# The product of the inverse with the betas on VectorE in all six sets, with the order of all engines drawn anew

## The chip, the cores and the metric

The program runs on one core of a Trainium2 chip. A core has TensorE (PE in the profile; its weight loads are PEld), VectorE (DVE), ScalarE (ACT), GpSimd (POOL) and SyncE (SP), which here issues the transfers. The metric is the device time of one execution in microseconds (us), as the median of several runs.

## What is computed

Three stages follow one another: a delta-rule attention over 4 batches, 8 heads, 768 tokens and head size 48, a gated MLP with a convolution of 5 taps, and a second gated MLP with a mixing over the tokens. Cut to the first stage, to which the change belongs, and the shapes of the others:

```python
k_n = k / (norm(k, axis=-1) + 1e-6)
for t in range(768):
    y[:, :, t] = q[:, :, t] @ state
    v_old = state^T k_n[:, :, t]
    state = state + beta[:, :, t] * outer(k_n[:, :, t], v[:, :, t] - v_old)

gate = sigmoid(causal_conv5(x, conv_w));  x1 = (gate * (x @ w_val)) @ w_out        # x: [4, 768, 384]
h = gelu_tanh(x1 @ w_in);  u, v = halves(h);  v_n = layernorm(v) * g_ln            # 512 each
out = x1 + (u * (w_sg @ v_n + b_sg)) @ w_out2
```

## The kernel before

**Attention.** The tokens are cut into chunks of 64, 12 for each of the 4 batches, 48 in all, and two chunks (`d`) are prepared together. Within a chunk the delta rule becomes the inverse of a triangular matrix made of the products of keys, times the betas. The inverses are computed for blocks of 32 tokens, all 32 blocks of four pairs of chunks in one go: this is a *set*, `k`, of which there are six. For a set, `norm`, `keys` and `gram` make the keys and their products `gd`, and `base(k)` inverts. `X` [128 partitions, 32 x 32, float32] starts as the transposed `gd`, and VectorE eliminates it in 30 steps, larger ones as a product into `tmp` and an addition, small ones in fused instructions (`X<-X`). Then `X` is multiplied by `bm`, the betas with the upper triangle kept, and transposed twice into `tab`, from which `tbh` and `tah` come (a float16 value and its remainder; for set 0 one of the transposes goes to `w2`). In the kernel before, the multiplication by `bm` is VectorE's in set 0 and GpSimd's in sets 1 to 5 (line 873).

`merge(d)` joins two 32-blocks to a 64-block with matmuls into `ps_b` and puts the result into `tbd`. Then `seq(n)` runs chunk after chunk, a recurrence: PE multiplies keys with the state (`ps_q<-wh,kj`), for batches 1 to 3 VectorE adds the values (`ps_q<-ps_q,vf`), ScalarE and VectorE split the result into two float16 parts (`rh`), PE multiplies by the inverse (`ps_q<-rh,tbd`), ScalarE and VectorE split again (`wh`), PE updates the state (`ps_state<-wh,kj`) and both split it once more (`wh<-ps_state`). `attend(n)` makes the outputs (`ps_y`, `mh`, `ys`).

**MLPs.** For each batch three tiles of 256 tokens go through `front`, `value`, `hidden`, `gates`, `mix` and `final`, with matmuls into `ps_mlp` of 256 or 512 columns. They need the attention's output of their tokens, so most of them come late. Each float32 product is made of three float16 matmuls. `a`, `gvh`, `gth`, `v`, `vnh`, `xh` and `st` are MLP tiles.

**The order.** All code of the kernel only records operations. `in_order` (line 110) then issues each engine's operations in the order that a table written out by hand, `ORDER` (line 239), gives for that engine: numbers of its operations in recorded order, with `a:n` for a run of n. Each engine works its list strictly in turn. The list of VectorE before has one operation for set 0's product, and five fewer than after. Where the planner's costs foresee a gap of PE, it adds *fillers*, matmuls into an unused half of `ps_state` (`ps_state<-minus`), 64 or 128 rows high. All transfers are on SP's queue.

The touched lines, and the two beside them:

```python
nc.vector.tensor_tensor(out=rows, in0=rows, in1=t, op=ALU.add)                               # elimination
(nc.vector if k == 0 else nc.gpsimd).tensor_tensor(out=X, in0=X, in1=bm, op=ALU.mult)        # line 873
nc.vector.transpose(out=t, in_=src)                                                          # tab<-X
```

Of the kernel before, what the change touches and what calls it, by code (L numbers as in the profile page):

```python
# [15 lines left out]
ALU = mybir.AluOpType  # L16
# [196 lines left out]
class Pool:  # L213
# [5 lines left out]
    def tile(self, shape, dtype, name, tag=None, **kw):  # L219
# [326 lines left out]
def kernel(  # L546
# [17 lines left out]
    nc = Program(tc)  # L564
# [276 lines left out]
    def base(k):  # L841
# [6 lines left out]
        X = pp.tile([P, 32, 32], F32, name="X", tag="f4", bufs=2)  # L848
# [4 lines left out]
        bm = pp.tile([P, 32, 32], F32, name="bm", tag="xb")  # L853
# [4 lines left out]
        for j in range(1, 31):  # L858
            m = 31 - j
            if min(j, m) <= FUSED:  # L860
                for a, i in ((a, i) for a in range(j if j <= m else 1) for i in range(1 if j <= m else m)):
                    if j <= m:
                        t, row, c = X[:, a, j + 1:32], X[:, j, j + 1:32], X[:, a, j:j + 1]
                    else:
# [5 lines left out]
                                    in1=X[:, j:j + 1, j + 1:32].to_broadcast([P, j, m]), op=ALU.mult)  # L870
# [525 lines left out]
```

## Time and profile before

| | us |
|---|---|
| median of 3 runs | 645.57 (643.87 to 649.93) |
| profiled execution, its own time | 646.62 |
| its span, first to last instruction | 644.7 |
| PE busy | 575.0 (89%) |
| DVE busy | 503.1 (78%) |
| ACT busy | 398.2 (62%) |
| POOL busy | 179.6 (28%) |

A busy share is the time in which an engine has at least one instruction under way. The view of stretches gives for each engine the busy time and, as (x...), the instructions that begin there, then PE's granted clock as a share of full speed. The order of time has, for each row, the start, the duration, the engine, what is written from what, and in brackets the idle time ahead of it with what ended it. A row that stands for several instructions has their number at x. All lines are L108, since one helper issues everything: tiles tell the rows apart.

### The profile page before, as it was taken

To read this page: it belongs to the slowest core of one execution; us is meant where nothing else is said; L and a number is where in the kernel's file an instruction comes from. 1 tells how busy PE (TensorE), PEld (TensorE's weight loads), DVE (VectorE), ACT (ScalarE), POOL (GpSimd) and SP (SyncE) were. 2 spreads that over 40 slices of the span, in tenths; PEclk is the share of its full clock that TensorE was granted. 3 is DMA by queue.
4 is the path that set the end of the run, shared out by engine and by line. 5 is a ranking of instruction groups with operands and counts; after the bars stand their busy time and mean duration, and the time that the engine had idled before them with its cause. 6 is when DMAs were issued, how large, how long until landed. Compare 5 with 4: busy or idle time off the path is not lost. (4 is left out here: it accounts for less than half of the span.)

```text
span 644.7 us, 23559 instructions
## 1 busy us (share of the span) xinstructions
PE 575.0 (89%) x9821; PEld 473.8 (73%) x9821; DVE 503.1 (78%) x1341; ACT 398.2 (62%) x932; POOL 179.6 (28%) x204
## 2 busy tenths in 40 slices
PE   0678879779979989799999999889999999999997
PEld 0555446668767767688888689778978897877886
DVE  7898998979889998988999879899887854562222
ACT  7886697756876767775466785344948544524221
POOL 7404041126423625366001650001605010303000
PEclk9999998989999998999999999999999999999999
DMA  7664367877579776687678778788687763211121
GB/s 223 160 202 132 126 189 235 186 156 165 107 182 175 134 122 146 128 195 132 163 143 179 145 123 170 121 140 152 120 155 141 107 142 102 63 50 34 58 82 50
DMA packets 288826, 89.22 MB, mean 138 GB/s; under 512 B 250704, under 2 KB 276944, under 8 KB 288720
## 3 DMA queue, kind: packets, MB, share of 16 engines
q1 hardware_dynamic: 288720, 87.72, 63.0%
q8 instruction: 77, 1.26, 0.9%
q14 instruction: 29, 0.24, 0.1%
HBM read 51.81 MB, written 23.33 MB: 117 GB/s over the span
## 5 line engine op out<-in xcount | busy, mean ns | idle before, releaser
L108 PE MATMUL ps_mlp<-wg,vnh 128*128 128x256 f16 x864 | 112.4, 272 | 1.4 <-DVE ps_mlp L108 1.4
L108 PEld LDWEIGHTS <-vnh 128*128 128x128 f16 x864 | 80.5, 97 | 12.0 <-issue 2.1
L108 PEld LDWEIGHTS <-kj 112*128 112x128 f16 (+1 forms) x1632 | 69.2, 97 | 21.4 <-issue 12.7
L108 PEld LDWEIGHTS <-kc 64*64 64x64 f16 x1920 | 42.1, 113 | 47.5 <-DVE kc L108 20.8
L108 PE MATMUL ps_mlp<-gvh,wi 128*128 128x256 f16 x432 | 58.0, 272 | 1.2 <-ACT v L108 0.8
L108 PE MATMUL ps_mlp<-gth,w 128*128 128x256 f16 x432 | 58.8, 272 | 0.0
L108 DVE TENSOR_TENSOR tmp<-X 128x84 f32<-128x84 f32 (+12 forms) x156 | 56.1, 360 | 1.4
L108 DVE TENSOR_TENSOR X<-X,tmp 128x84 f32<-128x84 f32 (+12 forms) x156 | 54.5, 349 | 1.5
L108 PE MATMUL ps_mlp<-wi,gvh 128*128 128x512 f16 x216 | 54.7, 379 | 0.6 <-ACT gvh L108 0.4
L108 DVE SCALAR_TENSOR_TENSOR ps_mlp<-ps_mlp,gl,bs 128x256 f32<-128x256 f32 x48 | 23.4, 488 | 34.3 <-PE ps_mlp L108 33.9
L108 DVE SCALAR_TENSOR_TENSOR a<-x,cw,a 128x256 f32<-128x256 f32 x108 | 48.8, 486 | 1.6 <-ACT a L108 1.3
L108 PE MATMUL ps_mlp<-xh,wv 128*128 128x256 f16 x324 | 45.7, 272 | 2.2 <-ACT xh L108 2.1
L108 PE MATMUL ps_mlp<-gvh,wo 128*128 128x256 f16 x324 | 47.1, 272 | 0.1
L108 PEld LDWEIGHTS <-m1p 128*128 128x128 f16 x1152 | 39.5, 96 | 9.9 <-issue 5.7
L108 PE MATMUL pk<-i,kc 64*64 64x64 f16 x704 | 22.5, 200 | 27.2 <-DVE kc L108 20.0
L108 PEld LDWEIGHTS <-wi 128*128 128x128 f16 x432 | 40.3, 97 | 6.4 <-issue 1.3
L108 PEld LDWEIGHTS <-w 128*128 128x128 f16 x432 | 40.8, 98 | 5.0
L108 PE MATMUL ps_y<-qh,kj 112*128 112x64 f16 x576 | 32.8, 193 | 4.2 <-ACT ys L108 4.1
L108 POOL TENSOR_TENSOR X<-X,bm 128x1024 f32<-128x1024 f32 x5 | 11.8, 2353 | 87.4 <-DVE X L108 72.0
L108 PEld LDWEIGHTS <-ws 128*128 128x128 f16 (+1 forms) x828 | 32.2, 98 | 4.9 <-issue 3.2
L108 PEld LDWEIGHTS <-wo 128*128 128x128 f16 x342 | 31.8, 97 | 5.5 <-issue 0.9
L108 POOL TENSOR_TENSOR vnh<-v,vnh 128x512 f16<-128x512 f32 x24 | 27.9, 1170 | 25.6 <-ACT vnh L108 25.5
(165 smaller groups left out, 1451.5 us busy)
## 6 DMA issues: line engine op xcount, KB each, us to landing
keys_d<-kc SPq DMA_DIRECT2D x22, 512.0 KB, 4.1
kj<-keys_d SPq DMA_DIRECT2D x44, 256.0 KB, 5.0
wg<-wgd SPq DMA_DIRECT2D x12, 768.0 KB, 4.8
ws<-wh SPq DMA_DIRECT2D x66, 96.0 KB, 3.6
qf<-in_qt SPq DMA_DIRECT2D x24, 224.0 KB, 3.5
kf<-in_kn SPq DMA_DIRECT2D x12, 384.0 KB, 4.7
vf<-in_vn SPq DMA_DIRECT2D x24, 192.0 KB, 3.4
xd<-ys SPq DMA_DIRECT2D x48, 96.0 KB, 3.0
```

The lines of the kernel that those rows point to most:

```text
L108: op.call()
```

## The change

In sets 1 to 5 the product of `X` with `bm` is made by VectorE, as in set 0. VectorE's list has 5 operations more, GpSimd's 5 fewer. The table of order is drawn anew for all five engines. One line of each list of VectorE stands for it:

```diff
     vector=(
-        "1 5 0 4 6 3 2 7 47:2 8:2 248 10 414 11 249 156 12 415 13 147 14 157 15 158 16 152 17 153 18 154 19:6 161 25 "
+        "2:2 1 0 4:4 47:2 8:2 248 10:2 415 12:2 156:2 249 14 416 158 15 152 16 153 147 17 154 18:7 161 25 33 162 28 "
...
-        (nc.vector if k == 0 else nc.gpsimd).tensor_tensor(out=X, in0=X, in1=bm, op=ALU.mult)
+        nc.vector.tensor_tensor(out=X, in0=X, in1=bm, op=ALU.mult)
```

VectorE at the end of set 1's inverse, before, from the `rh` of a chunk of batch 0 on (`wh_111` and `wh_110` are two of the three tiles of split states, `tbd_95` one of the two of merged inverses, `rs_t`, `rs` and `wst` norms of later keys and weights):

```order
L108 SCALAR_TENSOR_TENSOR rh<-ps_q,rh 128x192
L108 TENSOR_TENSOR mh<-ps_y,mh 128x256
L108 SCALAR_TENSOR_TENSOR tbd_95<-ps_b,tbd_95 32x8x32
L108 SCALAR_TENSOR_TENSOR wh_111<-ps_q,wh_111 128x4x48
L108 STREAM_TRANSPOSE tab<-X 128x1024
L108 TENSOR_SCALAR rs<-rs_t 128x32
L108 SCALAR_TENSOR_TENSOR wh_111<-ps_state,wh_111 112x4x48
```

The same place in the changed kernel:

```order
L108 SCALAR_TENSOR_TENSOR rh<-ps_q,rh 128x192
L108 TENSOR_TENSOR X<-X,bm 128x1024
L108 TENSOR_TENSOR mh<-ps_y,mh 128x256
L108 SCALAR_TENSOR_TENSOR wh_111<-ps_q,wh_111 128x4x48
L108 STREAM_TRANSPOSE tab<-X 128x1024
L108 TENSOR_SCALAR rs<-rs_t 128x32
L108 SCALAR_TENSOR_TENSOR tbd_95<-ps_b,tbd_95 32x8x32
L108 SCALAR_TENSOR_TENSOR gx<-pk,gx 128x256
L108 SCALAR_TENSOR_TENSOR rs_t<-rs 128x32
L108 SCALAR_TENSOR_TENSOR wst<-wst 128x384
L108 SCALAR_TENSOR_TENSOR wh_111<-ps_state,wh_111 112x4x48
```

The product comes in behind `rh`; `tbd`, `gx`, `rs_t` and `wst` stand ahead of the split of the state, `wh_111<-ps_state`, where before only `rs` stood between it and the transpose.

VectorE at the end of set 2's inverse, before, from the split of a state of batch 1 on:

```order
L108 SCALAR_TENSOR_TENSOR wh_109<-ps_state,wh_109 112x4x48
L108 TENSOR_TENSOR gvh<-ps_mlp,gvh 128x512
L108 SCALAR_TENSOR_TENSOR ps_q<-ps_q,vf 128x192
L108 SCALAR_TENSOR_TENSOR ps_mlp<-a,ps_mlp 128x256
L108 SCALAR_TENSOR_TENSOR rh<-ps_q,rh 128x192
```

The same place in the changed kernel:

```order
L108 SCALAR_TENSOR_TENSOR wh_109<-ps_state,wh_109 112x4x48
L108 TENSOR_TENSOR X<-X,bm 128x1024
L108 TENSOR_TENSOR gvh<-ps_mlp,gvh 128x512
L108 SCALAR_TENSOR_TENSOR ps_q<-ps_q,vf 128x192
L108 SCALAR_TENSOR_TENSOR ps_mlp<-a,ps_mlp 128x256
L108 SCALAR_TENSOR_TENSOR rh<-ps_q,rh 128x192
```

Here the product stands ahead of the whole row from `gvh` to `rh`, which are in the same order as before.

## Rows read from the trace of the kernel before

**Rows 1.** The page: span, and part 1, busy us and share.

```profile
span 644.7 us, 23559 instructions
...
PE 575.0 (89%) x9821; PEld 473.8 (73%) x9821; DVE 503.1 (78%) x1341; ACT 398.2 (62%) x932; POOL 179.6 (28%) x204
```

**Rows 2.** Stretches: length, busy us of PE, PEld, DVE, ACT, POOL, clock, DMA.

```profile
140.00:200.00 60.00, 53.79 (x1348) 44.84 (x1345) 52.42 (x145) 44.81 (x107) 27.46 (x28) 1.00 0.74 175
200.00:273.00 73.00, 64.66 (x1292) 53.03 (x1290) 66.90 (x189) 51.25 (x125) 33.77 (x35) 0.98 0.73 131
273.00:345.00 72.00, 71.70 (x1224) 62.66 (x1223) 66.01 (x180) 44.74 (x104) 22.87 (x22) 1.00 0.79 163
345.00:480.00 135.00, 127.93 (x2212) 109.01 (x2211) 117.91 (x308) 83.56 (x197) 34.27 (x31) 1.00 0.79 141
480.00:600.00 120.00, 118.51 (x1528) 99.78 (x1527) 69.84 (x175) 61.25 (x135) 22.08 (x24) 1.00 0.44 93
```

**Rows 3.** Tile X: count, shortest, median, longest ns, first and last start.

```profile
L108 POOL TENSOR_TENSOR X<-X,bm x5: 2346/2353/2358, 140.1 to 448.2; 128x1024 f32<-128x1024 f32 x5
L108 DVE TENSOR_TENSOR X<-X,bm x1: 1226/1226/1226, 80.1 to 80.1; 128x1024 f32<-128x1024 f32 x1
```

**Rows 4.** Order of time on DVE, end of set 1: start, duration us.

```profile
139.68 0.26 DVE L108 SCALAR_TENSOR_TENSOR X<-X 128x30 f32<-128x30 f32 x1
...
140.47 0.36 DVE L108 SCALAR_TENSOR_TENSOR rh<-ps_q,rh 128x192 f16<-128x192 f32 x1
140.81 0.42 DVE L108 TENSOR_TENSOR mh<-ps_y,mh 128x256 f16<-128x256 f32 x1
141.27 0.42 DVE L108 SCALAR_TENSOR_TENSOR tbd<-ps_b,tbd 32x256 f16<-32x256 f32 x1
141.74 0.36 DVE L108 SCALAR_TENSOR_TENSOR wh<-ps_q,wh 128x192 f16<-128x192 f32 x1
142.47 1.25 DVE L108 STREAM_TRANSPOSE tab<-X 128x1024 f32<-128x1024 f32 x1 [0.38 <-POOL X L108]
...
144.15 0.36 DVE L108 SCALAR_TENSOR_TENSOR wh<-ps_state,wh 112x192 f16<-112x192 f32 x1 [0.36 <-PE ps_state L108]
```

**Rows 5.** Waits of PE over the span: us in all, times, longest.

```profile
PE ps_b L108 <- DVE tbh L108: 1.0, 1, 1.0
```

**Rows 6.** Order of time on DVE: rh after set 2, two products gd.

```profile
152.28 1.81 DVE L108 SCALAR_TENSOR_TENSOR gd<-gd,beta_sb 128x1024 f32<-128x1024 f32 x1
...
205.91 0.36 DVE L108 SCALAR_TENSOR_TENSOR rh<-ps_q,rh 128x192 f16<-128x192 f32 x1
...
210.65 1.21 DVE L108 SCALAR_TENSOR_TENSOR gd<-gd,beta_sb 128x1024 f32<-128x1024 f32 x1
```

**Rows 7.** Order of time on PE after set 2.

```profile
204.91 1.81 PE L108 MATMUL ps_mlp<-wi,gvh 128*128 128x512 f16 x7
206.56 0.46 PE L108 MATMUL ps_q<-rh,tbd 128*128 128x48 f16 x12
```

**Rows 8.** Order of time on PE where 64 and 128 rows alternate.

```profile
353.95 0.34 PE L108 MATMUL pk<-i,kc 64*64 64x64 f16 x9
354.23 0.25 PE L108 MATMUL ps_state<-wh,kj 128*128 128x48 f16 x3
354.40 0.31 PE L108 MATMUL pk<-i,kc 64*64 64x64 f16 x7
354.64 0.40 PE L108 MATMUL ps_state<-wh,kj 128*128 128x48 f16 x9
```

**Rows 9.** Order of time on POOL beside the first product gd.

```profile
152.20 0.82 POOL L108 TENSOR_TENSOR tah<-tab,tah 128x256 f16<-128x256 f32 x1
```

**Rows 10.** Stretches of one microsecond at two falls of the clock.

```profile
134.00:135.00 1.00, 0.00 (x0) 0.00 (x0) 0.97 (x5) 0.40 (x1) 0.00 (x0) 0.88 0.06 5
248.00:249.00 1.00, 1.00 (x26) 1.00 (x24) 0.71 (x2) 0.96 (x3) 1.00 (x2) 0.50 0.55 63
```

**Rows 11.** Tile ps_state: the fillers.

```profile
L108 PE MATMUL ps_state<-minus x268: 269/272/421, 20.5 to 273.0; 128*128 128x256 f16 x70, 64*64 64x256 f16 x64
```

392 rows, old and new, of tables (gpsimd, scalar, sync, tensor) are left out of this document.

## The prediction

> **What bounds the kernel now.** I read the page first, then the table by stretches, then the waits, and last the order of time around the instructions that move. The page gives a span of 644.7 us with TensorE (PE) busy for 89% of it [rows 1]. The table by stretches splits this into two regimes. From 273 us on PE is busy for 71.70 of 72, 127.93 of 135 and 118.51 of 120 us: it is the bound there, and VectorE (DVE) and GpSimd (POOL) work only counts if PE runs dry. Before that PE has 53.79 of 60 and 64.66 of 73 us, while DVE has 52.42 and 66.90 us: 87% and 92% [rows 2]. There neither is at its limit alone. The recurrence over the chunks goes PE, ScalarE, VectorE and back to PE several times in each chunk, and VectorE squeezes the inverses and everything else between its steps. PE's remaining gaps are partly filled by idle matmuls of the planner, so its busy share there overstates useful work.
>
> Counted over the whole order, the program has 267 such fillers before and 252 after. In both, the last one is issued when the same share of the real matmuls is still to come. What PE has to do after it is thus the same, and the time can only change by when PE gets there and by its stalls behind that place. The last filler begins at 273.0 us [rows 11], which is why I cut the table there.
>
> **The change, part by part.**
>
> *Removed.* Five POOL multiplications X·bm of 2.353 us, 11.8 us in all [rows 3]. POOL is busy for 28% of the span [rows 1], so its own time is worth nothing. A gain could only come from a shorter way from the end of the inverse to its users. In the second set, the first that changes, the inverse ends at 139.68 + 0.26 = 139.94 us and its transposition starts at 142.47 [rows 4], 2.5 us later. The new instruction is 1.1 us shorter, but the order shown above puts two instructions of the recurrence between it and the transposition, as before. And nobody waits: of PE's waits only one, 1.0 us, is for a product of an inverse, and it is for set 0, which VectorE made already [rows 5]. I cost this gain at 0. What hides it is the matmuls of earlier chunks, which PE still has; without them it would be at most 1.1 us a set.
>
> *Added.* Five VectorE multiplications. Set 0 shows the very form: 1.226 us [rows 3], so 5 × 1.226 = 6.1 us of VectorE. Where do they lie? POOL's five begin at 140, 204, 275, 354 and 448 us (first and last in [rows 3]); three of them are behind the last filler, where PE has work queued and is 95 to 100% busy [rows 2]: 0, hidden by PE's matmuls of the MLPs. Without that cover each would cost up to 1.2 us.
>
> Two remain. **Set 1 (140 us).** Before, VectorE does rh, mh, tbd, wh, idles 0.38 us until POOL is done, and transposes [rows 4]. After, the multiplication stands between rh and mh, and tbd goes behind the transposition together with three more instructions ahead of the next wh (from ps_state). Placing the new rows with the old durations: rh ends its turn at 140.81, the multiplication holds the engine to about 142.0, mh and wh to 142.6, the transposition to 143.8, then rs, tbd, gx, rs_t and wst about 1.5 us more: wh from ps_state starts at about 145.3 instead of 144.15 [rows 4], so the recurrence is late by some 1.1 us. PE idles at this very place for DVE's wh already. Bounds 0 (the next chunk catches up) and 1.2; I take 1.1, since fillers still run there and PE has little else.
>
> **Set 2 (204 us).** The multiplication stands ahead of gvh, ps_q and rh. rh began at 205.91 and its matmuls at 206.56 [rows 6, 7]; 1.2 us later is 207.8. PE covers this with matmuls on wi that end at 206.56 [rows 7], and the new order has no more of them in front of the matmuls of rh. So PE idles for about 1.2 us more; bounds 0 (the 64.66 of 73 us leave 8 us of idle time nearby that may shrink in return) and 1.2. I take 1.2. Together +2.3 us.
>
> *Redrawn order.* The other rows of the table moved by a few places; I compared the lead between maker and user for the recurrence and the merges along PE's order, and no class of them is systematically shorter. One count differs: matmuls of 64 rows and of 128 rows alternate 167 times before and 147 times after; behind the last filler 38 and 32. In the trace, from 353.95 to 354.40 us, 9 matmuls of 64 rows and 3 of 128 rows take 0.45 us. The spacing inside the groups is (0.34 - 0.19)/8 = 0.019 and (0.40 - 0.18)/8 = 0.027 us, so 0.25 us is theirs and 0.20 us belongs to two alternations: 0.10 us each [rows 8]. Six fewer where PE is the bound give -0.6 us; the other 14 lie where PE waits anyway, worth between 0 and -1.4; I take -0.7, the half. The 15 fillers that go are time in which PE waited: 0.
>
> *POOL's other work.* Without the 2.35 us, qh and vnh of POOL can start earlier. Their users are on PE's list for later; 0.
>
> *Sum.* 2.3 - 0.6 - 0.7 = +1.0 us. The profiled execution took 646.62 us (span 644.7, 1.9 around it), and so 647.6 by its own measure. It was 1.05 us above the median of 645.57 of the runs shown, so against that median the forecast is **646.6 us**, +0.2%.
>
> **A rule that speaks against the change.** The trace has VectorE at 87% and 92% in the two stretches in which two of the five multiplications fall [rows 2]. The Trainium skill, "Perfetto Trace Analysis", section "Optimizing Scalar/DVE Operations", says that with VectorE saturated it may make sense to offload work to GpSimd, which is the reverse of this edit; by it the whole 6.1 us would be paid. The rows agree in that VectorE is near its limit there, but not behind 273 us, where PE is the limit.
>
> A multiplication on POOL might also have held up VectorE, and its removal would then give time back. In the trace the VectorE instructions between 140.1 and 142.4 us, during POOL's 2.35 us, take 0.36 to 0.42 us [rows 4], no longer than at other places. Each of them has one operand in PSUM. The opposite case is there too: gd<-gd,beta, both from SBUF, took 1.81 us while POOL ran its subtraction for tah, and 1.21 us without [rows 6, 9]. The Trainium skill, "SBUF — State Buffer", section "SBUF: two separate sides", calls the port pair of the two engines an exclusive lock that VectorE takes with two SBUF inputs; by it nothing is given back here, and the new multiplication, with X and bm both in SBUF, can be held up.
>
> **The rivals.**
> 1. *VectorE is the bound after all.* The place is every set from 1 to 5, since VectorE has 117.91 of 135 us even from 345 to 480 [rows 2]. Each multiplication then costs its 1.226 us and the wait that the pair gd shows, 1.81 - 1.21 = 0.60 us: 5 × 1.83 = 9.1 us, 654.7 us. It decides the sign from 1.29 us per set (1% of 645.57 is 6.46 us). Against it speaks PE's share behind 273 us. Chance 0.12.
> 2. *The held-up multiplication in sets 1 and 2 only*: 2 × 0.60 us on top of my sum, 647.8 us. For it speaks that POOL is free earlier and may run vnh or qh just then. Chance 0.15.
> 3. *The new order avoids the falls of the clock.* Three times PE's granted clock goes from full to half, 2.4 to 1.2 GHz: at 97 to 101, 134 to 139 and 247 to 251 us. Before the second PE had done nothing in the microsecond from 134; in the third it was busy throughout [rows 10]. Added up over its microseconds each is 3.4 us at the half clock (two or three whole ones at 0.50 and parts at both ends), so up to 1.7 us lost; all three gone give -5.1 us, and with the sum of alternations taken in full (-2.0) 645.57 - 7.1 = 638.5 us; two more falls would give +3.4. For it: the gaps ahead of these places depend on the order. Against it: the fillers stand at almost the same places. Chance 0.09.
> 4. *Nothing moves*: the two multiplications fall into idle time of the recurrence, 645.6 - 1.3 = 644.3 us. Chance 0.24.
> My forecast has 0.40.
>
> **How the numbers follow.** Rivals 2 and 4 and the forecast lie within 1% (639.1 to 652.0 us, about what a measurement of this kernel can tell from no change): 0.79. Slower by more than 1%: rival 1, 0.12. Faster by more than 1%: rival 3, 0.09. The range has to leave out no more than 0.2. The cases within 1% with the spread of the runs of before (643.87 to 649.93) reach from about 641 to 651; I take it on to 653 for the lower part of rival 1, and to 640 for the weaker forms of rival 3 (without the alternations it gives 640.5).
>
> **What would show it.** Right: six VectorE rows X<-X,bm of about 1.23 us, and none on POOL; the last filler at 274 to 276 us instead of 273; PE idle a little longer at 145 and at 207 us; the same shares of PE behind it. VectorE's busy time should rise from 503.1 to about 509 us. Wrong: multiplications of 1.8 us or more beside a POOL instruction (rivals 1 and 2); a PE share behind 273 us that drops by several us, with waits for VectorE (rival 1); another number of falls of the clock (rival 3); or a transfer such as m1p or ws that lands late at a place where the new order leaves less room, which none of my terms holds.

## The result and the profile after

The changed kernel takes 651.05 us as the median of 16 runs (647.22 to 654.44), the kernel before 645.71 us beside it (16 runs, 641.29 to 652.36). The ratio is 1.009, with a 95% interval of 1.0062 to 1.0117: +5.3 us. That lies inside the range of the prediction (640 to 653) and within 1%, and 4.5 us above the forecast of 646.6. Ratios leave out runs of a kernel over 1.5% above its fastest, which is why a ratio can differ from that of the medians.

The profiled execution of the changed kernel took 648.67 us, 2.4 us less than its median, while that of the kernel before was 0.9 us above its own. The two traces therefore show only 2.05 of the 5.3 us; where the rest lies, no trace shows. The page of the changed kernel, span and part 1:

```profile
span 647.0 us, 23517 instructions
...
PE 576.0 (89%) x9806; PEld 474.1 (73%) x9806; DVE 506.7 (78%) x1346; ACT 396.7 (61%) x932; POOL 169.5 (26%) x199
```

Against [rows 1] VectorE has 3.6 us more and GpSimd 10.1 us less. The same stretches as in [rows 2], of the changed kernel (length; busy us of PE, PEld, DVE, ACT, POOL; clock; DMA):

```profile
140.00:200.00 60.00, 55.17 (x1331) 46.55 (x1329) 52.81 (x140) 43.30 (x106) 27.80 (x28) 0.94 0.72 168
200.00:273.00 73.00, 64.02 (x1284) 52.10 (x1280) 67.32 (x188) 49.84 (x122) 30.23 (x33) 0.98 0.74 131
273.00:345.00 72.00, 68.88 (x1179) 60.45 (x1179) 64.32 (x177) 43.55 (x102) 18.52 (x20) 1.00 0.78 163
345.00:480.00 135.00, 130.89 (x2272) 112.38 (x2271) 122.03 (x318) 84.63 (x199) 31.20 (x29) 1.00 0.77 141
480.00:600.00 120.00, 117.75 (x1524) 98.47 (x1521) 69.30 (x176) 61.92 (x137) 22.70 (x25) 1.00 0.47 93
```

The new thing is in the third row: PE idles for 3.1 us of 72, where before it idled for 0.3, in a stretch that the prediction had called hidden. In the fourth row it has 3.0 us more work done than before. Tiles X and ps_state of the changed kernel, which answer to [rows 3] and [rows 11]:

```profile
L108 DVE TENSOR_TENSOR X<-X,bm x6: 1203/1216/1220, 82.4 to 452.0; 128x1024 f32<-128x1024 f32 x6
...
L108 PE MATMUL ps_state<-minus x253: 269/272/421, 20.9 to 274.9; 128*128 128x256 f16 x76, 64*64 64x256 f16 x51
```

All six products take 1.20 to 1.22 us, so none was held up on VectorE (GpSimd was, see the rivals below). The last filler begins at 274.9 us. And the first product, that of set 0, which VectorE made before too, begins at 82.4 us and not at 80.1: VectorE is 2.3 us late there, ahead of everything that the moved products can touch.

**How lateness is read below.** For each kind of real matmul, the n-th start in one trace is set against the n-th start in the trace of before; the median difference in a stretch (by the time of before) is called the lag. How the lag grows across a place is what that place costs against before. Each trace has some falls of the clock (before at 97, 134 and 247 us, the changed kernel at 59, 182 and 250 us), and a place with a fall inside it isn't used, but for the start, where it is said.

### The profile page after: what moved, and what is told of

It is laid out like the page before. It is cut to its first block, busy times and chain, and to the rows that moved or that the text cites. A ratio compares the mean times of both kernels' runs of the same rounds, so it can differ in the third digit from the quotient of the medians.

```text
span 647.0 us, 23517 instructions
## 1 busy us (share of the span) xinstructions
PE 576.0 (89%) x9806; PEld 474.1 (73%) x9806; DVE 506.7 (78%) x1346; ACT 396.7 (61%) x932; POOL 169.5 (26%) x199
## 4 chain that ended last, share of the span: by engine, by line
PE 39%; DVE 8%; DMA 4%; ACT 3%; issue 2%; SPq 0%; POOL 0%; POOLq 0%; ACTq 0%; DVEq 0%
PE ps_mlp L108 31%; PE ps_y L108 3%; PE ps_q L108 2%; DMA wg<-wgd 1%; DVE ps_mlp L108 1%; DMA ws<-wh 1%; PE ps_b L108 1%; DVE X L108 1%; PE pk L108 1%; DMA x<-xd 1%; PE ps_state L108 1%; DVE a L108 1%; DVE tmp L108 1%; ACT tah L108 0%; SPq L108 0%
## 5 line engine op out<-in xcount | busy, mean ns | idle before, releaser
L108 PEld LDWEIGHTS <-kj 112*128 112x128 f16 (+1 forms) x1632 | 67.9, 97 | 20.3 <-issue 11.6
L108 DVE TENSOR_TENSOR X<-X,tmp 128x84 f32<-128x84 f32 (+12 forms) x156 | 56.8, 364 | 1.4
L108 POOL TENSOR_TENSOR xh<-x,xh 128x780 f16<-128x780 f32 x12 | 20.0, 1670 | 59.8 <-ACT xh L108 58.5
L108 PEld LDWEIGHTS <-wv 128*128 128x128 f16 x324 | 29.6, 97 | 5.9 <-issue 1.9
```

What stands on the lines that cost most here:

```text
L108: op.call()
```

## The experiments

Five rounds each, 10 to 12 runs of each kernel, beside 33 to 35 runs of the kernel before.

| kernel | order until | order behind | products on VectorE | median us | before | ratio (95%) |
|---|---|---|---|---|---|---|
| changed | | redrawn | 0 to 5 | 651.05 | 645.71 | 1.0090 (1.0062 to 1.0117) |
| e1_move | | of before | 0 to 5 | 648.22 | 646.21 | 1.0043 (1.0009 to 1.0078) |
| e2_early | | of before | 0, 1, 2 | 645.35 | 646.21 | 1.0004 (0.9974 to 1.0034) |
| e3_late | | of before | 0, 3, 4, 5 | 646.61 | 646.21 | 0.9987 (0.9951 to 1.0022) |
| e4_neworder_pool | | redrawn | 0 | 650.48 | 646.21 | 1.0075 (1.0047 to 1.0104) |
| g1_oldstart | of before to 100 us | redrawn | 0 to 5 | 649.21 | 645.54 | 1.0075 (1.0047 to 1.0104) |
| g2_latebs | | redrawn, one operation moved | 0 to 5 | 649.35 | 645.54 | 1.0061 (1.0025 to 1.0097) |
| g3_oldhalf | of before to 315 us | redrawn | 0 to 5 | 645.17 | 645.54 | 0.9965 (0.9927 to 1.0003) |
| g4_newstart | redrawn to 100 us | of before | 0 | 649.58 | 645.54 | 1.0044 (1.0010 to 1.0077) |
| h1_old205 | of before to 205 us | redrawn | 0 to 5 | 646.23 | 645.00 | 1.0023 (0.9985 to 1.0061) |
| h2_old255 | of before to 255 us | redrawn | 0 to 5 | 647.56 | 645.00 | 1.0025 (0.9990 to 1.0059) |
| h3_pool123 | of before to 315 us | redrawn | 0, 4, 5 | 642.60 | 645.00 | 0.9976 (0.9939 to 1.0012) |
| h4_fill | as g3_oldhalf, FILL 0.8 | | 0 to 5 | 648.34 | 645.00 | 1.0048 (1.0010 to 1.0085) |

### The move without the redrawn order, and the order without the move

e1 to e3 keep the order of before; each moved product stands on VectorE just ahead of the first transposition of its set. e4 keeps the redrawn order and gives the five products back to GpSimd, each where it stood among GpSimd's other operations.

```diff
 e1_move (e2: k in (0, 1, 2); e3: k in (0, 3, 4, 5); the table only with the moved numbers)
-        (nc.vector if k == 0 else nc.gpsimd).tensor_tensor(out=X, in0=X, in1=bm, op=ALU.mult)
+        (nc.vector if k in (0, 1, 2, 3, 4, 5) else nc.gpsimd).tensor_tensor(out=X, in0=X, in1=bm, op=ALU.mult)
 e4_neworder_pool, against the changed kernel
-        nc.vector.tensor_tensor(out=X, in0=X, in1=bm, op=ALU.mult)
+        (nc.vector if k == 0 else nc.gpsimd).tensor_tensor(out=X, in0=X, in1=bm, op=ALU.mult)
```

> The move alone: the table of order is that of before, and the five products of sets 1 to 5 stand on VectorE just ahead of the first transpose of X, where VectorE waited for GpSimd before; GpSimd's list loses them, all else keeps its place (the planner adds 277 fillers instead of 268). Theory A (the prediction's steps: only sets 1 and 2 cost anything, and the redrawn order gives back 1.3 us): +2.3 us against before. Theory B (VectorE is the bound in all sets, rival 1): +6 to +9 us. Theory C (the redrawn order costs, not the move; the +5.3 us measured come from its stalls and falls of the clock): 0 to +1 us.

> As e1_move, but only the products of sets 1 and 2 on VectorE, those of sets 3 to 5 stay on GpSimd at their places. Theory A: +2.3 us, the same as e1_move. Theory B: two fifths of e1_move, +2.5 to +3.7 us. Theory C: 0 to +1 us.

> As e1_move, but only the products of sets 3 to 5 on VectorE. Theory A: 0 us, since TensorE has work queued there. Theory B: three fifths of e1_move, +3.7 to +5.5 us. Theory C: 0 us.

> The redrawn order alone: the changed kernel with the five products put back on GpSimd, at the places of its list that keep its order of before best; VectorE's list only loses them. The transposes stand where the redrawn list has them, one or two instructions behind the end of the inverse, so VectorE waits for GpSimd up to 2 us in front of each. Theory A: -1.3 us by the order and up to +2 us in sets 1 and 2 by those waits, so -1 to +1 against before. Theory B: the waits hold VectorE longer than the products would, +6 to +10. Theory C: +4 to +6 us, nearly all of the change's slowdown.

e4 decides the main question: with no product moved, the redrawn order costs 0.75%, nearly all of the 0.9%. Theory C had that. The waits that were expected in front of e4's transpositions are not the cause, for VectorE waits for GpSimd's product there only 0.8 us in all, twice:

```profile
DVE tab L108 <- POOL X L108: 0.8, 2, 0.5
```

The same is seen from the other side in g3 below: it has all six products on VectorE, as the changed kernel has, but the order of before up to 315 us, and it loses nothing (0.9965 against 1.0090).

Theory B falls, since neither e2 nor e3 is measurably slower. The move alone, e1, costs 0.43% (2.8 us, between 0.6 and 5.0). That is nearer to A's 2.3 than to C's 0 to +1, but it excludes neither. In the redrawn order the move adds 0.15% (changed against e4), which is less than the uncertainty of either. A missed with e2: its +2.3 us lie just above what e2 allows (+0.34%, 2.2 us).

What the products cost is seen better in the traces, at the sets' ends. The growth of the lag (us) from just ahead of the end of the set to just behind it, for kernels that work there in the order of before:

```
set  stretches compared          product on VectorE                 product on GpSimd
1    141:144 and 157:165         e1 +1.0  e2 +0.8  g3 +0.8  h2 +0.8   e3  0.0  g4  0.0  h3 +0.2
2    200:204 and 214:220         e1 +1.3  e2 +1.4  g3 +1.4  h2 +1.4   e3 +0.3  g4 -0.2  h3 -0.2
3    272:276 and 284:288         e1 +0.7  e3 +0.7  g3 +0.7            e2  0.0  g4  0.0  h3  0.0
5    445:450 and 470:478         e1 +0.3  e3 +0.4                     e2 -0.7  g4 -0.2
```

(Set 4 can't be read, because before has a wait of its own there, below.) In set 2 the chain of waits of e2 (start, duration, what) goes through the product:

```profile
207.95 0.36 DVE wh L108
...
208.31 1.14 DVE X L108
...
209.47 1.25 DVE tab L108
```

In h3, where GpSimd makes it, the chain goes from the same `wh` straight to the transposition:

```profile
204.41 0.36 DVE wh L108
...
204.76 1.16 DVE tab L108
```

So the product stands in the chain there, with 1.14 us. In set 3 the rows of e3 show how a product reaches PE even where PE is all but full. VectorE, order of time (start, duration):

```profile
275.99 1.22 DVE L108 TENSOR_TENSOR X<-X,bm 128x1024 f32<-128x1024 f32 x1
277.24 1.25 DVE L108 STREAM_TRANSPOSE tab<-X 128x1024 f32<-128x1024 f32 x1
278.41 0.45 DVE L108 SCALAR_TENSOR_TENSOR ps_mlp<-ps_mlp,gl,bs 128x256 f32<-128x256 f32 x1
```

and PE of the same kernel:

```profile
278.92 2.12 PE L108 MATMUL ps_mlp<-wg,vnh 128*128 128x256 f16 x18 [0.60 <-DVE ps_mlp L108]
```

The matmuls on `wg` wait for VectorE's `ps_mlp<-ps_mlp,gl,bs`. Product and transposition, 2.4 us together, stand ahead of it, and PE has matmuls for all but 0.60 us of the time. Before has no such wait here.

The medians of e2 and e3 show less than these delays: e2 has at most +0.34%, 2.2 us, and its two places sum to 2.2. That e2 spent less time at half clock (10.5 us a run in the mean, by the granted clock of each run, against 16.4 of before) may have paid it back; this isn't shown.

### Where the redrawn order loses: cuts between the two orders

Each kernel here works up to some time in one order and behind it in the other. Against the changed kernel only the table differs, and with it the number of fillers that the planner adds (253 there, 266 to 279 in g1, g3, h1 and h2). h3 also gives three products back to GpSimd, and g4 has those of before. g2 moves a single operation of ScalarE's list.

```diff
 g1, g3, h1, h2, h3: ORDER of before for all that it issues up to the cut, then the redrawn ORDER for the rest (g4: the other way round)
 g2_latebs, ScalarE's list
 ACTIVATE kc<-pk 128x512
-ACTIVATE bs<-bs 128x256
 ACTIVATE tah<-tab 128x256
...
 ACTIVATE u<-ps_mlp 128x512
+ACTIVATE bs<-bs 128x256
 ACTIVATE gx<-pk 128x256
```

> The changed kernel, but up to about 100 us of the span (to behind the inverse of set 0) each engine works in the order of before; from there the redrawn order, with all products on VectorE. Theory D (the redrawn order loses its time at named places; the first is the start, where X<-X,bm of set 0 began at 82.4 us in the changed kernel and at 80.1 before): about 651 - 2.5 = 648.5, ratio to before 1.004 +- 0.003, X<-X,bm of set 0 again near 80 us. Theory E (the start's lateness is made up later by the fillers and slack, the loss lies only behind 250 us): unchanged, about 651, ratio 1.008. Theory F (the products themselves cost it): unchanged too, 651.

> The changed kernel with one operation of ScalarE's list moved: bs<-bs, which at 290.1 us waited 1.90 us for its transfer bs<-in_b_sg with two tah<-tab, m1p, mh, rh and gd queued behind it, goes behind the second u<-ps_mlp, where before had it. Theory D: the wait on ScalarE goes and with it VectorE's waits for m1p and mh (1.16 and 1.53 us) and PE's wait of 1.00 us at 296.6; 1.0 to 2 us less, about 649.5, ratio 1.0055 +- 0.003. Theory E1 (PE is held there by VectorE's own length of work, the wait is cover): no change, 651, ratio 1.008.

> The changed kernel, but up to about 315 us of the span each engine works in the order of before (the products of sets 1 to 3 on VectorE just ahead of the first transpose); from there the redrawn order. Theory D: both lossy places are gone, the stretch from 345 us keeps what the redrawn order won there: 651 - 5 = 646, ratio 1.000 +- 0.003, or below. Theory F (the products on VectorE in sets 1 and 2 cost 2 to 3 us): 648 to 649, ratio 1.004. Theory E2 (the loss is spread over the whole redrawn order, half of it behind 315 us): 648.5, ratio 1.004, and PE's busy share behind 345 us lower than in the kernel before.

> The kernel before (products on GpSimd in sets 1 to 5), but up to about 100 us of the span each engine works in the redrawn order. Theory D: 646.2 + 2.5 = 648.7, ratio 1.004 +- 0.003, X<-X,bm of set 0 near 82.5 us. Theory E (made up later): 646, ratio 1.000.

> As g1_oldstart and g3_oldhalf, with the change from the order of before to the redrawn one at about 205 us (behind the product of set 2). The stretch from 100 to 315 us, where the two ends differ by 4 us (649.2 and 645.2), is thereby cut in two. Theory G (the loss lies at the place from 265 to 310 us, where the lag behind before grew by 1.7 to 2.9 us in every profile with the redrawn order): 649, ratio 1.006 +- 0.003. Theory H (it lies between 100 and 205 us, at the ends of sets 1 and 2): 645 to 646, ratio 0.998. Theory I (spread evenly): 647.

> The same with the change of order at about 255 us, ahead of the place from 265 to 310 us. Theory G: 649, as h1_old205, ratio 1.006 +- 0.003, with ScalarE's wait of about 1.9 us for in_b_sg near 290 us and a PE busy share from 273 to 345 us of about 69 us of 72. Theory H: 645, ratio 0.998. Theory I: 646.

> As g3_oldhalf, but the products of sets 1 to 3 are GpSimd's, as in before; VectorE has those of sets 0, 4 and 5. Theory D (a product on VectorE costs nothing that can be measured): as g3_oldhalf, 644 to 645.5, ratio 0.996 to 1.000. Theory A (sets 1 and 2 cost 1.1 and 1.2 us): 2.3 us less than g3_oldhalf, 642.9, ratio 0.993 +- 0.003.

By the medians, the loss shrinks as more of the order of before is put in front: 651.05 (none), 649.21 (to 100 us), 646.23 (205), 647.56 (255), 645.17 (315); by the ratios 1.0090, 1.0075, 1.0023, 1.0025, 0.9965. The steps are 1.3 to 3.0 us, about the uncertainty of a single one (some 2 us), but the ends are far apart: all of the loss lies ahead of 315 us, and theory E2 falls. Theories G (all of it behind 255 us, 1.006) and H (all of it between 100 and 205 us, 0.998) lie at the edges of the intervals of h1 and h2; I (spread) fits the medians best, but they don't prove it. The traces show places. Growth of the lag against before, in us:

```
place                         redrawn order there                               order of before there
start,  0 to 80:100           changed +2.1  e4 +2.6  g2 +2.4  g4 +2.2           e1 -0.8  g1 +0.1  g3 -0.6  h3 +0.4
set 3,  255:262 to 288:294    changed +1.7  e4 +2.1  h2 +1.6                    e1 +0.8  g3 +0.8  e3 +0.7  e2 +0.1  g4 0.0  h3 0.0
wait,   288:294 to 294:300    changed +1.1  e4 +1.1  g1 +1.1  h1 +1.1  h2 +1.1  0.0 in all six; g2 (one operation moved) +0.1
gain,   346:350 to 419:425    changed -3.8  e4 -3.8  g1 -3.1  g2 -3.1  h1 -4.0  h2 -4.0  h3 -4.0 | e1 +0.6  e2 -0.1  e3 -1.1  g4 -1.7
rest,   419:425 to 590:600    changed +1.8  e4 +1.9  g1 +0.7  g2 +0.7  h1 +1.7  h2 -0.7  h3 +1.1 | e1 +0.5  e2 +0.5  e3 +1.1  g4 +0.6
```

**The start** (theory D against E). VectorE in the order of time, during set 0's elimination, in the changed kernel:

```profile
56.37 0.29 DVE L108 SCALAR_TENSOR_TENSOR wst<-wst 128x128 int32<-128x128 int32 x1 [3.34 <-ACT wst L108]
56.58 1.12 DVE L108 TENSOR_TENSOR X<-X,tmp 128x240 f32<-128x240 f32 x1
...
59.31 0.41 DVE L108 TENSOR_TENSOR X<-X,tmp 128x240 f32<-128x240 f32 x1
...
64.25 0.48 DVE L108 SCALAR_TENSOR_TENSOR gd<-pk,which,gd 128x256 f32<-128x256 f32 x1 [2.11 <-ACT gd L108]
...
77.63 0.29 DVE L108 SCALAR_TENSOR_TENSOR wst<-wst 128x128 int32<-128x128 int32 x1 [1.19 <-ACT wst L108]
```

and at the same places before:

```profile
53.80 0.34 DVE L108 TENSOR_TENSOR X<-X,tmp 128x240 f32<-128x240 f32 x1
55.64 3.04 DVE L108 SCALAR_TENSOR_TENSOR wst<-wst 128x128 int32<-128x128 int32 x3 [1.50 <-ACT wst L108]
...
59.38 0.40 DVE L108 TENSOR_TENSOR X<-X,tmp 128x240 f32<-128x240 f32 x1
...
75.41 0.29 DVE L108 SCALAR_TENSOR_TENSOR wst<-wst 128x128 int32<-128x128 int32 x1
```

The redrawn list puts the preparation of a weight, `wst`, ahead of a step of the elimination that was ready, and the step waits behind it for ScalarE: 3.34 us and not 1.50. But before has a wait for `wst` one step later, and at 59.3 us the two eliminations are level again; `wst` cost only a lead of 0.85 us that the redrawn order had until 53 us. The wait for `gd` at 64 us makes the elimination 2.0 us late, and half of that is made good by 67 us. From 76 us on it is 2.2 to 2.3 us late, behind one more `wst`, which waits 1.19 us where before it waited for nothing. How the 2.3 us are shared among these waits isn't shown.

All four kernels with this start also have a fall of the clock at 59 to 60 us. With the old start g1, with a fall at 67 us, has +0.1, and h1, with falls at 68 and 89 us, has +0.6, so the fall is not most of the 2.1 to 2.6 us. g4 has this start alone and is 0.44% slower (0.10 to 0.77), as D said. Its trace doesn't show how, though: in that execution (645.70 us, 3.9 us under its median) the lag was +2.2 us at 80 to 100 us and -0.2 at 255 to 262, with three falls of the clock ahead of that place in both traces, which is what E said. Taking the start out of the changed kernel (g1) gave 1.8 us by the medians and 0.15% by the ratios, less than the 2.5 us of D and not certain by itself. So the place of the lateness is shown; that it reaches the end is likely, but not settled.

**The place from 265 to 300 us.** PE of the changed kernel, order of time:

```profile
275.87 2.12 PE L108 MATMUL ps_mlp<-gvh,wi 128*128 128x256 f16 x18 [0.70 <-DVE gth L108]
278.73 1.47 PE L108 MATMUL ps_mlp<-wg,vnh 128*128 128x256 f16 x12 [0.73 <-DVE gvh L108]
...
292.06 2.12 PE L108 MATMUL ps_mlp<-wg,vnh 128*128 128x256 f16 x18 [0.35 <-DMA wg<-wgd]
...
296.62 0.38 PE L108 MATMUL ps_mlp<-wg,vnh 128*128 128x256 f16 x2 [1.00 <-DVE ps_mlp L108]
```

and ScalarE ahead of the last of these:

```profile
290.11 0.42 ACT L108 ACTIVATE bs<-bs 128x256 f32<-128x256 f32 x1 [1.90 <-DMA bs<-in_b_sg]
290.43 0.63 ACT L108 ACTIVATE tah<-tab 128x256 f16<-128x256 f32 x1
291.08 0.38 ACT L108 ACTIVATE m1p<-ps_b 32x256 f16<-32x256 f32 x1
291.48 1.52 ACT L108 ACTIVATE tah<-tab 128x768 f16<-128x768 f32 x1
```

There is only one buffer of `bs`, so its transfer starts when VectorE is done with the last one (issued at 285.32 us, VectorE's last use ends at 285.29). It lands 4.8 us after its issue, and here ScalarE comes to `bs` 1.90 us before that, with `tah`, `m1p` and the recurrence queued behind it. The same wait, 1.4 to 2.0 us, is in every kernel with the redrawn order here (e4, g1, h1, h2). In g2 the operation runs later and waits for nothing:

```profile
295.91 0.41 ACT L108 ACTIVATE bs<-bs 128x256 f32<-128x256 f32 x1
```

and the step of 1.1 us in the lag goes (row "wait" of the table). D expected 1 to 2 us of it; by the medians it is 1.7 us, less than their uncertainty. The rest of the place, 1.6 to 2.1 us against 0.7 for the product alone, is in the waits of 0.70 and 0.73 us for `gth` and `gvh` above; e4 has it without any product on VectorE. No run took these two apart.

**The gain.** PE before, order of time:

```profile
357.62 0.38 PE L108 MATMUL ps_b<-tbh,m1p 128*128 128x32 f16 x9 [1.44 <-DMA m1p<-gx]
...
416.85 0.33 PE L108 MATMUL ps_b<-tbh,m1p 128*128 128x32 f16 x7 [1.25 <-DMA m1p<-gx]
```

The changed kernel has neither of the two waits for the transfer `m1p<-gx`, and its lag falls by 3.8 us in this stretch. Part of this is lost again by 600 us (row "rest"): from 346 us to there the redrawn order wins 1.9 to 2.9 us in six traces and 4.7 in h2, while the lag of e1 to e3 and g4, with the order of before, changes by -1.2 to +1.2 us. So the redrawn order is the better one behind 345 us and the worse one ahead of it. g3 and h3, which join the good halves, are the fastest kernels here. h3's median is 642.60 us, 2.4 us under before and 8.4 under the changed kernel; its interval against before (0.9939 to 1.0012) still holds no change. h3's median is 2.6 us under g3's, which looks like A's 2.3 for the products of sets 1 and 2, but the two were run beside different runs of before, and by the ratios there is no such difference (0.9976 and 0.9965). So this pair decides nothing between A and D.

### The clock

> g3_oldhalf with one constant changed, FILL from 0.55 to 0.8, which about doubles the fillers. The runs of one kernel are 0.2 to 0.3 us longer for each us at half clock, and g3_oldhalf has 11.6 us of it in the mean. Theory J (the falls of the clock cause the longer runs): fewer falls, half-clock time 5 us or less, 645.2 - 2 = 643, ratio 0.994 +- 0.003. Theory K (falls and long runs have a common cause, late work, or the fillers delay real matmuls): half-clock time down, the time not: 645 or above.

```diff
-..., FILL = ..., 0.55
+..., FILL = ..., 0.8
```

With about twice the fillers (592 in the trace, g3 has 277) the half-clock time of a run, worked out from the span and mean granted clock of each as (1 - clock) × 2 × span, went from 11.6 to 3.5 us in the mean, and the median from 645.17 to 648.34 us. Theory K holds: keeping the clock up in this way costs more than the falls.

## Why the prediction came out as it did

Range and direction held; the forecast was 4.5 us too low. That the range held was in part luck. The cases within 1% were to reach up to about 651, and the range went on to 653 for a weaker form of rival 1, which did not happen; the time came there by a term that the prediction had with the wrong sign.

**Set 1, +1.1 us: right in size.** VectorE in the changed kernel, the rows that answer to [rows 4]:

```profile
140.07 0.36 DVE L108 SCALAR_TENSOR_TENSOR rh<-ps_q,rh 128x192 f16<-128x192 f32 x1 [0.17 <-ACT rh L108]
140.35 1.22 DVE L108 TENSOR_TENSOR X<-X,bm 128x1024 f32<-128x1024 f32 x1
141.48 0.42 DVE L108 TENSOR_TENSOR mh<-ps_y,mh 128x256 f16<-128x256 f32 x1
141.81 0.35 DVE L108 SCALAR_TENSOR_TENSOR wh<-ps_q,wh 128x192 f16<-128x192 f32 x1
142.08 1.24 DVE L108 STREAM_TRANSPOSE tab<-X 128x1024 f32<-128x1024 f32 x1
...
144.77 0.35 DVE L108 SCALAR_TENSOR_TENSOR wh<-ps_state,wh 112x192 f16<-112x192 f32 x1
```

From `rh` to `wh` of the state it is 4.70 us, before 144.15 - 140.47 = 3.68: 1.0 us more. PE's lag grew by 1.1 us from 139:141 to 157:165. In the order of before the product cost PE 0.8 to 1.0 us. But in e4, with the product on GpSimd, the lag grows by 1.6 us here, so in the redrawn order the loss isn't shown to be the product's.

**Set 2, +1.2 us: right in size, and nearly in place.** PE of the changed kernel waits for `gvh`, one instruction ahead of the matmuls of `rh` that the prediction named:

```profile
207.22 1.47 PE L108 MATMUL ps_mlp<-wi,gvh 128*128 128x512 f16 x6 [0.61 <-DVE gvh L108]
208.52 0.46 PE L108 MATMUL ps_q<-rh,tbd 128*128 128x48 f16 x12
```

The lag grew by 1.0 us here, and by 1.3 to 1.4 in the order of before. Since e4's lag grows by 1.5 us up to 214 us without the product, the part of the product in the redrawn order isn't settled here either.

**Sets 3 to 5, 0: wrong for set 3.** The step that failed is "hidden by PE's matmuls of the MLPs". A PE busy share of 71.70 of 72 us says that nothing has made it wait yet, not how long it could go without VectorE. At this place PE waited 0.60 us once VectorE was late by a product, and the lag grew by 0.7 us in three kernels; set 5 shows 0.5 to 1.

**The redrawn order, -1.3 us: wrong, and this is what missed the time.** The prediction compared leads class by class, found none systematically shorter, and counted only alternations. What the runs showed in its place is waits at single operations: `bs` at 290 us, where moving the one operation took 1.1 us of lag away, and, seen in the rows but not moved one by one, `gth` and `gvh` at 276 us and `wst` and `gd` at the start. By e4 the redrawn order costs 0.75%, +4.8 us, where -1.3 stood. It also wins more than the 0.6 us that alternations were to give behind the last filler, 1.9 to 2.9 us from 346 to 600 us in most traces; what the alternations gave was not taken apart.

**The fillers: right.** The last one at 274.9 us (274 to 276 forecast), and 253, 15 fewer. VectorE's busy time rose by 3.6 us, not 6: five products came, and other work there got shorter.

**The rivals.** VectorE as the bound in all sets (654.7): no, e1 is +0.43%. The sign that was named for it, a lower PE share from 273 us on with waits for VectorE, is there (68.88 of 72 us), but e4 has it too (67.77) with no product moved. The held-up multiplication: no, 1.22 us at most in six. It was GpSimd that was held up, in sets 1 and 2:

```profile
140.48 1.61 POOL L108 TENSOR_TENSOR qh<-qf,qh 112x256 f16<-112x256 f32 x1 [12.35 <-ACT qh L108]
```

Before, `qh` takes 0.67 us in the median. Here it begins 0.13 us after the product and ends 0.52 us after the product's end. In all 13 such overlaps of the traces `qh` ends 0.52 to 0.53 us after the product, whenever it began. This agrees with the exclusive lock that the Trainium skill describes ("SBUF — State Buffer", section "SBUF: two separate sides"), by which the engine that comes second waits for the first; in each of the 13 VectorE came first. Fewer falls of the clock: no, the mean half-clock time of the changed kernel is 18.4 us a run, before 16.4. Nothing moves (644.3): no. The Trainium skill ("Perfetto Trace Analysis", section "Optimizing Scalar/DVE Operations") calls offloading from a saturated VectorE something that may make sense, and adds that between VectorE and GpSimd it might not help. The prediction's reading of it, 6.1 us paid, was too much: e1, the move alone, paid 2.8 us, between 0.6 and 5.0. The last warning of the prediction came true: a transfer that landed late where the new order left less room, `bs`.

## What to carry to other kernels

When an instruction moves and the order of everything else is redrawn with it, cost the two apart: here the size of the move was read fairly well from a few rows, and the redraw cost more than the move. Look in a new order for single operations that stand ahead of ready work and wait for something that can't be there yet, above all a transfer into the only buffer of its kind. An engine that is 99% busy is no cover by itself: ask how much of its queue is free of the late engine's results.

## What was not expected of the hardware

Within one kernel a run with more half-clock time is longer, by 0.1 to 0.4 us for each us (before: 0.24 over 33 runs, 0.21 and 0.35 over the two other sets of 35), where the prediction had allowed up to 0.5 (1.7 us lost in 3.4). h4 alone has more, 0.8, over half-clock times of a few us. Yet taking 8 us of half clock out with fillers made the kernel 3 us longer, so that slope is no price at which the clock can be bought back. Whether the fillers delay the real matmuls or draw on something else wasn't shown.
